# Storing the sums u to DRAM with all 128 rows, and writing the last tokens' row over one of them

## The chip, the cores and the metric

The program runs on one core of a Trainium2 chip. The metric is device time in microseconds (us) of one execution, the median of the runs shown. The engines that appear below are PE (TensorE, matmuls), PEld (its weight loads), DVE (VectorE), ACT (ScalarE), POOL (GpSimd) and SP (SyncE, whose queue issues nearly all DMAs of this kernel, in the order in which they are written). A DMA moves its bytes through up to 16 DMA engines of the core.

## The reference

Attention with two kinds of sparse mask, then a Fourier mixing layer, a normalisation and a feed-forward layer, for 8 batches of 576 tokens and 512 channels:

```python
scores = scale * np.matmul(q, k.transpose(0, 1, 3, 2))
scores = np.where(masks[None, :, :, :], scores, -1000000000.0)
attn = np.exp(scores - np.max(scores, axis=-1, keepdims=True))
x = attn / (np.sum(attn, axis=-1, keepdims=True) + 1e-09) @ v   # to (B, S, H * D)
...
X = np.fft.fft(x, axis=1)
X = np.fft.fft(X, axis=2)
mixed = np.real(X).astype(np.float32)
u = x + mixed
mu = np.mean(u, axis=-1, keepdims=True)
var = np.mean((u - mu) ** 2, axis=-1, keepdims=True)
un = (u - mu) / np.sqrt(var + 1e-06)
ch = np.maximum(un @ w_ch1, 0.0) @ w_ch2
return (u + ch).astype(np.float32)
```

The matrices `q`, `k`, `v` are (8, 8, 576, 64), `w_ch1` is (512, 2048) and `w_ch2` (2048, 512).

## The kernel before

For each batch there are four pairs of heads. A pair is loaded (`qk`, `vn`), its scores are made on PE, masked and exponentiated on DVE and ACT (`sm`, then `pbt` or `qk` as 16-bit parts), transposed by a DMA (`pT`, line 478) and multiplied with the values (PE, lines 490 and 497). The results are stored to DRAM (`xd`, lines 777, 779, 791). When the four pairs of a batch are there, the batch is loaded again in two orders of its tokens (`xa`, `xb`), and matrix products with cosines and sines (`A`, `B`) give the Fourier sum. Its symmetry lets one product serve a token and its mirror image, so the sums `u` come in two halves, "a" and "b", each in two tiles of 128 rows and 512 channels, and a third piece with the last 33 tokens and their mirrors.

The sums are what the change is about. Function `sums` writes them (line 1033 and above) and, for the first two tiles (`t` is 0 or 1), issues a "keep": line 1037 stores the "a" half with all 128 rows to its DRAM tensor `ud`, line 1038 stores the "b" half from row 1 to row 127. Row 0 of "b" is its own mirror and not wanted there. In its place comes the last of the 33 tokens: when the third piece is there (`t` is 2), the step "ux" writes it with a DMA of one row into row 0 of `ud` (line 1045), and the other 32 tokens of both kinds into a tensor that two batches share (lines 1048, 1049). For batches 0 to 2 (`DIRECT`) the sums are normalised from SBUF instead of from `ud`; there line 1044 also writes the row into row 0 of the SBUF tile.

The feed-forward layer takes 18 chunks of 256 rows. For each half of a chunk `u` is loaded (`ul`, line 1281, one buffer), normalised on DVE, POOL and ACT (lines 1075 to 1097), split in two 16-bit parts (`unp`, one buffer) and transposed by a DMA (`uT`, line 1099). Two matrix products follow on PE: `ph` (line 1307) with a relu on ACT (lines 1322, 1323) and a 16-bit remainder on POOL (line 1325), and `acc` (line 1346). DVE adds `u`, loaded once more (`uf`, line 1288), and line 1358 stores the output.

The order of all instructions is made before the program is built: each step is a generator that yields an `op` with an engine, an estimated duration, the rooms it takes and gives back and the names of events that it needs (`need`) or sets (`sets`). A planner picks the next step by estimated time and a priority. The engines then run in the order found; where data must be waited for, a wait on a semaphore is put before the instruction. An SP instruction that waits holds all of SP's queue behind it.

Of the kernel before, what the change touches and what calls it, by code (L numbers as in the profile page):

```python
# [19 lines left out]
B, H, S, D = 8, 8, 576, 64  # L20
# [12 lines left out]
DIRECT = P["dir"]  # L33
# [237 lines left out]
op = Op  # L271
# [3 lines left out]
def body(ctx: ExitStack, tc: tile.TileContext, a, out):  # L275
    nc = tc.nc
# [75 lines left out]
    ud = {key: dram.tile([128, DM], F32, name=f"ud{c}_{i}") for key, (c, i) in place.items()}  # L352
# [406 lines left out]
    def att_out(b, hp, po, eps, scale, xo=None):  # L759
# [4 lines left out]
        if xo is None:  # L764
            xo = apool.tile([128, 2 * NG2 * D], F32, tag="xo", name=f"xo{nm}", bufs=1)
        n = 9 if hp < 2 else 2 * NG2
        sums, vals = po[:, :, :, D], po[:, :, :, 0:D]
        rv = rs[:, 0:n].rearrange("p (a b) -> p a b", a=po.shape[1])
        V.tensor_scalar(rv, sums, eps, scale, op0=ALU.add, op1=ALU.bypass if scale is None else ALU.mult)
        V.reciprocal(rs[:, 0:n], rs[:, 0:n])  # L770
        rb = rv.rearrange("p a (b o) -> p a b o", o=1).to_broadcast([128, po.shape[1], po.shape[2], D])
# [189 lines left out]
    def products32(b, FD, sds, xa, xb):  # L961
# [34 lines left out]
        for t in range(3):  # L996
            r = 128 if t < 2 else 33
            yield op("T", 2.3, get="big" + (" u" if t < 2 else ""), need=" ".join(f"AT{g}_{b}" for g in range(5)), put="f6" if t == 2 else "", note=f"B{t} {b}")
            ps = psbig(f"B{b}_{t}")

            T.matmul(ps[:, 0:512], zerb, zero.to_broadcast([128, 512]), start=True, stop=False)
            both = ps[0:r, 0:512].rearrange("p (i k) -> p i k", i=2)
            for g, (c0, w) in enumerate(GROUPS):
                x = AT[0:w, g, 128 * t : 128 * t + r]
                k0, k1, st = cols[g]
                if g == 0:
                    T.matmul(ps[0:r, 0:257:4], x, tb[0:w, 0:65], start=False, stop=False)
                    T.matmul(ps[0:r, 260:509:4], x, tb[0:w, 1:64], start=False, stop=False)
                elif g < 3:
                    T.matmul(both[:, :, k0:k1:st], x, tb[0:w, c0 : c0 + w].rearrange("p (o k) -> p o k", o=1).to_broadcast([w, 2, w]), start=False, stop=False)  # L1010
                else:
                    T.matmul(both[:, :, k0:k1:st], x, tb[0:w, 257:767].rearrange("p (i k) -> p i k", i=2)[:, :, c0 - 257 : c0 - 257 + w], start=False, stop=False)
            T.matmul(ps[:, 0:512], zerb, zero.to_broadcast([128, 512]), start=False, stop=True)
            spawn(sums(b, t, r, xa, xb, ps[0:r, 0:257], ps[0:r, 256:513], "big"), bias=P["t2"] if t == 2 else None)

    def sums(b, t, r, xa, xb, R_, T_, room):
        tt_ = lambda e, o, x, y, op: e.tensor_tensor(out=o, in0=x, in1=y, op=op)
        for i in range(2):
            o = op("V", 0.92, put=room if i else "", sets="" if b not in DIRECT or not i else (f"u{b}a0", f"u{b}a1", "")[t], note=f"u{t} {b}", alt=None if room == "big" else dict(G=(1.4, P["Lu"])))
            yield o  # L1020
            if i == 0:
                if t < 2:
                    uu = mp.tile([128, 2, DM], F32, tag="u", name=f"u{b}_{t}", bufs=UB)
                    dst = [uu[:, 0], uu[:, 1]]
                else:
                    dst = [xa[0:33, 2], xb[0:33, 2]]
            u, x, lo_, hi_ = (dst[0], xa, R_, T_) if i == 0 else (dst[1], xb, T_, R_)
            if i and room == "big":
                tt_(on(o), u[:, 1:256], lo_[:, 1:256], x[0:r, t, 1:256], ALU.add)
                tt_(on(o), u[:, 0:257:256], hi_[:, 0:257:256], x[0:r, t, 0:257:256], ALU.add)  # L1030
            else:
                tt_(on(o), u[:, 0:257], lo_, x[0:r, t, 0:257], ALU.add)
            tt_(on(o), u[:, 257:512], hi_[:, 255:0:-1], x[0:r, t, 257:512], ALU.add)
        if t < 2:
            us[b, "a", t], us[b, "b", t] = dst
            yield op("S", 1.4, n=2, put="" if b in DIRECT else "u", sets="" if b in DIRECT else f"u{b}a{t} u{b}c{t}", note=f"keep {b} {t}")
            nc.sync.dma_start(ud[b, "a", t], dst[0])
            nc.sync.dma_start(ud[b, "b", t][1:128], dst[1][1:128])
        else:
            yield op("S", 0.4, n=6 if b in DIRECT else 4, put="f6 f6", sets=f"u{b}b0 u{b}b1" + (f" ux{b // 2}" if b % 2 else ""), note=f"ux {b}")  # L1040

            for i in range(2):
                if b in DIRECT:
                    nc.sync.dma_start(us[b, "b", i][0:1], dst[i][32:33])
                nc.sync.dma_start(ud[b, "b", i][0:1], dst[i][32:33])
            hb = 64 * (b % 2)
            ux = ud["x", b // 2]
            nc.sync.dma_start(ux[hb : hb + 32], dst[0][0:32])
            nc.sync.dma_start(ux[hb + 32 : hb + 64], dst[1][0:32])
# [427 lines left out]
```

## Time and profile before

| | |
|---|---|
| median of 3 runs | 1079.88 us (1077.25 to 1080.66) |
| the profiled execution | 1085.56 us |
| its span (first to last instruction) | 1083.8 us |
| PE busy | 958.7 us (88%) |
| DVE, ACT, POOL busy | 561.9, 455.5, 403.5 us |
| mean granted clock of PE | 0.932 of full speed |
| data moved by DMA | 131.23 MB, mean 121 GB/s |

The page cuts the span in 40 slices of 27.1 us and gives for each the busy share of the engines in tenths, the clock that PE was granted and the DMA traffic. The other views used below: the waits (who was idle, and what ended it), the timeline (instructions in order of time with the idle time before them), the chain of work that ended last, the DMA traffic of a stretch, and the busy time of all engines in a list of stretches.

### The profile page before, as it was taken

The numbers are of one execution on the slowest core, as the hardware profiler recorded it, in microseconds if no ns is written. First come the engines' busy times: TensorE is split into PE (matmuls) and PEld (weight loads), VectorE is DVE, ScalarE is ACT, GpSimd is POOL, SyncE is SP. The second block draws the span as 40 slices with busy tenths as digits, with TensorE's granted clock in tenths as the row PEclk, the third lists the DMA queues.
The fourth block names the chain that finished last, engine by engine and source line by source line (L and its number), as shares of the span: only waits on it lengthen the run. The fifth ranks groups of instructions, "written<-read, shape, count | busy, mean of one in ns | idle before, by whom it ended". The sixth has DMA issues, their size and how long they took to land.

```text
span 1083.8 us, 23857 instructions
## 1 busy us (share of the span) xinstructions
PE 958.7 (88%) x9930; PEld 665.8 (61%) x9930; DVE 561.9 (52%) x1040; ACT 455.5 (42%) x893; POOL 403.5 (37%) x389
## 2 busy tenths in 40 slices
PE   7676579896996998977999997899699979999998
PEld 6645464673675666644776665667466656676665
DVE  4777397752864586735873886378616311011000
ACT  3535464442563456534652565356413412222211
POOL 2321132432643373325441654174427323233211
PEclk8858798898998999988999999899889989999999
DMA  8845847607635646258535655674453051130110
GB/s 261 295 163 190 164 134 228 151 31 147 153 103 86 145 119 161 74 137 160 145 75 148 180 121 88 142 198 122 64 143 102 30 93 31 49 78 21 49 40 20
DMA packets 148156, 131.23 MB, mean 121 GB/s; under 512 B 104264, under 2 KB 114760, under 8 KB 148048
## 3 DMA queue, kind: packets, MB, share of 16 engines
q1 hardware_dynamic: 145488, 121.32, 44.6%
q0 software_dynamic: 2560, 8.39, 2.7%
q8 instruction: 78, 1.28, 0.5%
q14 instruction: 30, 0.25, 0.1%
HBM read 79.97 MB, written 28.33 MB: 100 GB/s over the span
## 4 chain that ended last, share of the span: by engine, by line
PE 39%; DMA 7%; DVE 5%; issue 2%; POOL 1%; ACT 1%; SPq 1%; POOLq 0%; DVEq 0%; ACTq 0%
PE acc L1346 18%; PE ph L1307 17%; DMA pT<-pbt 3%; DMA ud<-u 2%; DMA uT<-unp 1%; DVE E L837 1%; PE B L957 1%; DMA ul<-ud 1%; DMA qk<-in_qk 1%; DVE kt L436 1%; PE A L934 1%; PE o L490 0%; PE s L459 0%; DVE FD L837 0%; DMA pT<-qk 0%
## 5 line engine op out<-in xcount | busy, mean ns | idle before, releaser
L1307 PE MATMUL ph<-uT,W 128*128 128x256 f16 x3456 | 399.2, 275 | 12.2 <-DMA uT<-unp 11.6
L1346 PE MATMUL acc<-W,h 128*128 128x512 f16 x1728 | 400.3, 387 | 6.5 <-DVE uf L1354 6.1
L1307 PEld LDWEIGHTS <-W 128*128 128x128 f16 x3456 | 338.2, 99 | 65.2 <-issue 13.2
L1325 POOL TENSOR_TENSOR h<-hf,h 128x512 f16<-128x512 f32 x144 | 181.1, 1257 | 355.3 <-ACT h L1323 271.4
L1346 PEld LDWEIGHTS <-h 128*128 128x128 f16 x1728 | 168.4, 99 | 211.1 <-issue 32.7
L1322 ACT ACTIVATE hf<-ph 128x512 f32<-128x512 f32 x144 | 85.5, 594 | 262.8 <-PE ph L1307 221.8
L1323 ACT ACTIVATE h<-ph 128x512 f16<-128x512 f32 x144 | 85.0, 590 | 0.0
L1097 POOL TENSOR_TENSOR unp<-un,unp 128x512 f16<-128x512 f32 x36 | 44.0, 1222 | 107.5 <-ACT unp L1094 107.4
L1354 DVE SCALAR_TENSOR_TENSOR uf<-acc,cout,uf 128x512 f32<-128x512 f32 x36 | 26.4, 746 | 89.3 <-PE acc L1346 89.2
L436 DVE SCALAR_TENSOR_TENSOR kt<-qk,sc,kt 128x576 f16<-128x576 f32 (+1 forms) x40 | 46.4, 1198 | 31.8 <-ACT kt L421 29.6
L1088 DVE TENSOR_SCALAR un<-ul,mv,rstd 128x512 f32<-128x512 f32 x24 | 20.4, 849 | 80.5 <-POOL rstd L1081 78.8
L1094 ACT CAST unp<-un 128x512 f16<-128x512 f32 x36 | 22.2, 617 | 91.3 <-DVE un L1088 57.7
L1081 POOL TENSOR_TENSOR rstd<-mv,negh 128x1 f32<-128x1 f32 x36 | 23.6, 655 | 96.4 <-DVE mv L1078 66.1
L1075 DVE BATCH_NORM_STATS2 st<-ul 128x6 f32<-128x512 f32 x24 | 16.6, 690 | 75.3 <-DMA ul<-ud 75.3
L837 POOL TENSOR_TENSOR O<-xa,xb 128x1536 f32<-128x1536 f32 x8 | 31.0, 3878 | 15.4 <-DMA xb<-xd,ridx 15.4
L1060 ACT ACTIVATE pq<-B,fcm 128x128 f32<-128x128 f32 (+7 forms) x105 | 27.9, 378 | 19.0 <-PE B L957 8.0
L1181 PE MATMUL gram<-oneb,zero 128*128 128x128 bf16 x379 | 33.4, 261 | 0.0
L421 ACT ACTIVATE kt<-qk,sc 128x576 f16<-128x576 f32 (+1 forms) x40 | 29.3, 784 | 7.3 <-DVE sc L377 6.9
L1181 PEld LDWEIGHTS <-zero 128*128 128x128 bf16 x379 | 30.7, 121 | 2.1 <-issue 1.3
L497 PE MATMUL o<-vsx,pT 54*64 54x65 f16 x720 | 9.1, 208 | 25.2 <-DMA pT<-pbt 25.2
L471 ACT ACTIVATE sm<-sm 128x594 f32<-128x594 f32 (+1 forms) x20 | 16.2, 811 | 35.7 <-DVE sm L754 35.7
L752 DVE TENSOR_REDUCE mx<-sm 128x11 f32<-128x594 f32 (+1 forms) x32 | 29.1, 910 | 0.8
(215 smaller groups left out, 1132.8 us busy)
## 6 DMA issues: line engine op xcount, KB each, us to landing
qk<-in_qk SPq DMA_DIRECT2D x28, 592.0 KB
sa<-in_w SPq DMA_DIRECT2D x20, 512.0 KB
uf<-ud SPq DMA_DIRECT2D x36, 256.0 KB
out<-uf SPq DMA_DIRECT2D x36, 256.0 KB
ul<-ud SPq DMA_DIRECT2D x24, 256.0 KB
vn<-in_vl SPq DMA_DIRECT2D x10, 432.0 KB
W<-in_w SPq DMA_DIRECT2D x8, 512.0 KB
xd<-xo SPq DMA_DIRECT2D x16, 256.0 KB
```

The costliest lines, as they stand in the source:

```text
L421: A.activation(hi, src, AF.Copy, scale=f)
L436: V.scalar_tensor_tensor(out=lo, in0=src, scalar=f, in1=hi, op0=ALU.mult, op1=ALU.subtract)
L752: V.tensor_reduce(out=mx[:, 0:nb], in_=sm, axis=AX.X, op=ALU.max)
L837: tt_ = lambda e, o, x, y, op: e.tensor_tensor(out=o, in0=x, in1=y, op=op)
L1060: A.activation(dst, ps[0:r, c0:c1], AF.Copy, scale=cm[0:r])
L1097: on(o).tensor_tensor(out=unp[:, 1], in0=un, in1=unp[:, 0], op=ALU.subtract)
L1181: T.matmul(idle[-1][:, 0:128], zerb, oneb, start=False, stop=False)
L1307: T.matmul(ph[:, i, :], W1[:, 4 * (f0 // 512) + d, x, f0 % 512 : f0 % 512 + 128], self.uhl[y][:, d, :], start=(n == 0), stop=(n == 11))
L1322: A.activation(hf, ph, AF.Relu, scale=HS)
L1323: A.activation(hh, ph, AF.Relu, scale=HS)
L1325: G.tensor_tensor(out=hl, in0=hf, in1=hh, op=ALU.subtract)
L1346: T.matmul(self.acc[s], (hh, hl)[x][:, i, 128 * s : 128 * s + 128], W2[:, f, 1 - y, :], start=(f == 0 and n == 0), stop=(f == 15 and n == 2))
```

## The change

The "b" half is stored with all 128 rows, as the "a" half is. The row of the last token then goes over row 0 of a tensor that the store has written, so the step "ux" now needs the events that its two keeps are done; for batches 0 to 2 such an event is made, for the others the event was there already. No priority or other number is changed.

```diff
-            yield op("S", 1.4, n=2, put="" if b in DIRECT else "u", sets="" if b in DIRECT else f"u{b}a{t} u{b}c{t}", note=f"keep {b} {t}")
+            yield op("S", 1.4, n=2, put="" if b in DIRECT else "u", sets=f"kept{b}{t}" if b in DIRECT else f"u{b}a{t} u{b}c{t}", note=f"keep {b} {t}")
             nc.sync.dma_start(ud[b, "a", t], dst[0])
-            nc.sync.dma_start(ud[b, "b", t][1:128], dst[1][1:128])
+            nc.sync.dma_start(ud[b, "b", t], dst[1])
         else:
-            yield op("S", 0.4, n=6 if b in DIRECT else 4, put="f6 f6", sets=f"u{b}b0 u{b}b1" + (f" ux{b // 2}" if b % 2 else ""), note=f"ux {b}")
+            kept = f"kept{b}0 kept{b}1" if b in DIRECT else f"u{b}c0 u{b}c1"
+            yield op("S", 0.4, n=6 if b in DIRECT else 4, put="f6 f6", need=kept, sets=f"u{b}b0 u{b}b1" + (f" ux{b // 2}" if b % 2 else ""), note=f"ux {b}")
```

In the built program the order of PE, ACT and SP is the same as before, apart from line numbers (from line 1041 on they are one higher). What changes on SP is the size of the 16 stores and the waits. This is SP at batch 5, where the keep of the second tile and the step "ux" stand side by side (`ud_1_126`, `ud_1_128` are the "a" and "b" halves of the second tile, `u_1_9042` the sums, `xa` and `xb` hold the last tokens; DMAHW names are the semaphores of earlier DMAs). Before:

```order
L1037 DMA ud_1_126<-u_1_9042 128x512 [waits DMAHW1_49,Pool_49]
L1038 DMA ud_1_128<-u_1_9042 127x512 [waits DMAHW2_49,Pool_49]
L1045 DMA ud_0_127<-xa_8079 1x512 [waits DMAHW3_49,DMASW4_49,Pool_49]
L1045 DMA ud_1_128<-xb_8081 1x512 [waits DMAHW4_49,DMASW7_49,DVE_49]
L1048 DMA ud_0_133<-xa_8079 32x512 [waits DMAHW5_49]
L1049 DMA ud_0_133<-xb_8081 32x512 [waits DMAHW6_49]
L478 DMA_TRANSPOSE pT_3_9219<-pbt 128x12x128 [waits DMAHW7_49,DVE_49,PE_49]
```

And the same place of the changed kernel:

```order
L1037 DMA ud_1_126<-u_1_9042 128x512 [waits DMAHW1_49,Pool_49]
L1038 DMA ud_1_128<-u_1_9042 128x512 [waits DMAHW2_49,Pool_49]
L1046 DMA ud_0_127<-xa_8079 1x512 [waits DMAHW3_49,DMAHW6_49,DMASW4_49,Pool_49]
L1046 DMA ud_1_128<-xb_8081 1x512 [waits DMAHW2_49,DMAHW4_49,DMASW7_49,DVE_49]
L1049 DMA ud_0_133<-xa_8079 32x512 [waits DMAHW5_49]
L1050 DMA ud_0_133<-xb_8081 32x512
L478 DMA_TRANSPOSE pT_3_9231<-pbt 128x12x128 [waits DMAHW7_49,DVE_49,PE_49]
```

Nothing has moved; each one-row store has one more wait, for the 128-row store over whose row 0 it writes.

One place moves, on DVE in batch 7 near 867 us (and two instructions of POOL change places there). `uf` is the output of the feed-forward layer, the statistics `st` begin the normalisation of a freshly loaded `ul`. Before:

```order
L1088 TENSOR_SCALAR un_0_11957<-ul_0_11773,mv_0_11841,rstd_0_11892 128x512 [waits DVE_49]
L1354 SCALAR_TENSOR_TENSOR uf_0_11767<-acc_0_11489,cout,uf_0_11767 128x512 [waits DMAHW6_49,DMAHW3_49,PE_49]
L1075 BN_STATS st_1_12012<-ul_1_11969 128x6 [waits DMAHW1_49]
L1076 BN_AGGR mv_1_12013<-st_1_12012 128x2 [waits DVE_49]
L1078 TENSOR_SCALAR mv_1_12013<-mv_1_12013 128x1 [waits DVE_49]
```

And in the changed kernel:

```order
L1089 TENSOR_SCALAR un_0_11957<-ul_0_11773,mv_0_11841,rstd_0_11892 128x512 [waits DVE_49]
L1355 SCALAR_TENSOR_TENSOR uf_0_11767<-acc_0_11489,cout,uf_0_11767 128x512 [waits DMAHW6_49,DMAHW3_49,PE_49]
L1355 SCALAR_TENSOR_TENSOR uf_1_11836<-acc_1_11490,cout,uf_1_11836 128x512 [waits DMAHW4_49,DMAHW0_49,PE_49]
L1076 BN_STATS st_1_12015<-ul_1_11982 128x6 [waits DMAHW1_49]
L1077 BN_AGGR mv_1_12016<-st_1_12015 128x2 [waits DVE_49]
```

The second `uf` now stands before the statistics, which wait for the load of `ul`.

## Rows read from the trace of the kernel before

**Rows 1.** The page: the span and the line of busy time.

```profile
span 1083.8 us, 23857 instructions
PE 958.7 (88%) x9930; PEld 665.8 (61%) x9930; DVE 561.9 (52%) x1040; ACT 455.5 (42%) x893; POOL 403.5 (37%) x389
```

**Rows 2.** The view of waits, of PE: what was to run and what ended the idle time; us in total, times, longest in us.

```profile
PE o L497 <- DMA pT<-pbt: 25.2, 3, 10.3
...
PE ph L1307 <- DMA uT<-unp: 11.6, 1, 11.6
PE t L594 <- ACT pbt L585: 10.7, 1, 10.7
PE n L333 <- ACT jk L402: 8.8, 2, 6.6
PE s L459 <- ACT kt L421: 7.2, 1, 7.2
PE s L518 <- DMA qk<-in_qk: 6.5, 1, 6.5
PE acc L1346 <- DVE uf L1354: 6.1, 1, 6.1
...
PE s L459 <- DVE kt L436: 3.2, 3, 1.3
...
PE o L490 <- DMA pT<-qk: 1.6, 1, 1.6
```

**Rows 3.** The timeline of SP: start in us, how long the instruction held SP, line, operation, tiles.

```profile
96.98 16.85 SPq L1099 DMA_TRANSPOSE uT<-unp  x1
...
115.02 2.20 SPq L1099 DMA_TRANSPOSE uT<-unp  x1
...
236.96 13.80 SPq L1099 DMA_TRANSPOSE uT<-unp  x1
...
333.29 11.30 SPq L1099 DMA_TRANSPOSE uT<-unp  x1
...
447.56 0.26 SPq L1038 DMA_DIRECT2D ud<-u  x1
448.17 8.31 SPq L1045 DMA_DIRECT2D ud<-xa  x1
456.58 2.10 SPq L1045 DMA_DIRECT2D ud<-xb  x1
...
660.01 9.78 SPq L1045 DMA_DIRECT2D ud<-xa  x1
...
768.52 15.45 SPq L478 DMA_TRANSPOSE pT<-pbt  x1
...
858.74 0.61 SPq L1038 DMA_DIRECT2D ud<-u  x1
860.60 8.64 SPq L1045 DMA_DIRECT2D ud<-xa  x1
869.35 0.28 SPq L1045 DMA_DIRECT2D ud<-xb  x1
```

**Rows 4.** The transposes of line 1099 over the whole span: how long each held SP, shortest, median and longest in ns, and the first and last start in us.

```profile
L1099 SPq DMA_TRANSPOSE uT<-unp x36: 1231/1244/16851, 97.0 to 1002.1; - x36
```

**Rows 5.** The DMA view of the stretch from 853.6 to 856.3 us, in 40 slices of 0.07 us: the mean busy share of the 16 DMA engines in tenths, and the traffic. In it stand the keep of batch 7's first tile, line 1037 (issued at 853.6) and line 1038 (issued at 854.3).

```profile
DMA  0000000000005997999979520001002000000105
GB/s 0 0 0 0 0 0 0 0 0 0 0 0 212 394 394 303 425 394 425 364 273 455 182 61 0 30 0 30 0 0 30 0 0 0 30 0 30 30 0 30
```

**Rows 6.** A stretch just after the second keep of batch 3: start and end, length, busy us of PE, PEld, DVE, ACT and POOL with their counts, granted clock, mean busy share of the 16 DMA engines, GB/s.

```profile
450.00:456.00 6.00, 6.00 (x106) 4.09 (x92) 4.34 (x7) 1.29 (x2) 0.58 (x1) 1.00 0.07 27
```

**Rows 7.** The chain of work that ended last, between 555 and 582 us (batch 4's second keep and what follows): start, us, what.

```profile
559.30 17.66 DMA ud<-u
...
577.04 3.89 DMA pT<-qk
```

**Rows 8.** The timeline of the engines: start, us, engine, line, operation, tiles, and in brackets the idle time before it and what ended that.

```profile
105.56 1.16 POOL L1097 TENSOR_TENSOR unp<-un,unp 128x512 f16<-128x512 f32 x1 [9.81 <-ACT unp L1094]
...
122.82 5.14 PE L1307 MATMUL ph<-uT,W 128*128 128x256 f16 x24 [11.58 <-DMA uT<-unp]
...
255.06 0.62 ACT L1094 CAST unp<-un 128x512 f16<-128x512 f32 x1 [13.80 <-DMA uT<-unp]
...
348.85 0.62 ACT L1094 CAST unp<-un 128x512 f16<-128x512 f32 x1 [13.48 <-DMA uT<-unp]
...
661.05 0.76 DVE L475 SCALAR_TENSOR_TENSOR pbt<-sm,pbt 128x594 f16<-128x594 f32 x1
...
680.13 1.21 PE L497 MATMUL o<-vsx,pT 54*64 54x65 f16 x72 [8.96 <-DMA pT<-pbt]
...
787.50 1.21 PE L497 MATMUL o<-vsx,pT 54*64 54x65 f16 x72 [10.30 <-DMA pT<-pbt]
...
878.99 0.69 DVE L1075 BATCH_NORM_STATS2 st<-ul 128x6 f32<-128x512 f32 x1 [11.31 <-DMA ul<-ud]
```

**Rows 9.** Busy time in eight stretches, each just before or after one of the long waits of PE: columns as in Rows 6. The first, the last, and the sum over the eight.

```profile
105.30:111.20 5.90, 5.81 (x73) 5.27 (x73) 1.16 (x1) 2.55 (x5) 3.70 (x3) 0.55 1.70 50
...
880.90:885.40 4.50, 4.50 (x11) 1.57 (x11) 0.40 (x1) 1.69 (x3) 2.27 (x2) 0.50 0.39 105
sum 37.40, PE 35.91 PEld 22.83 DVE 19.21 ACT 12.30 POOL 13.70; mean PE 4.49 PEld 2.85 DVE 2.40 ACT 1.54 POOL 1.71
```

## The prediction

> **What bounds the kernel now.** I began with the page. PE is busy for 958.7 of 1083.8 us [rows 1], so what a change that leaves PE's work alone can win lies in the 125.1 us in which PE stands idle and in what PE's lower clock costs (below). PE's order is the same in the changed kernel, instruction by instruction, so I asked next what ended PE's idle time. The waits of PE [rows 2] show a few long ones, each met once, and they look unrelated: a transposed tile, a load of qk, an ACT copy, a DVE sum. Set side by side with SP's timeline they have one thing in common. Each stands within 30 us behind a keep (lines 1037 and 1038), and in that time one SP instruction holds the queue for 8 to 17 us: a transpose that takes 1.24 us in the median [rows 4] takes 16.85, 13.80, 11.30 or 15.45 us, a store of one row takes 8.31, 9.78 or 8.64 us [rows 3].
>
> Why SP is held is read from the traffic. The keep of 128 rows and the keep of 127 rows move nearly the same bytes. In Rows 5 the first of them shows as a burst: slices of 5 to 9 tenths on 16 engines, at up to 455 GB/s, over in some 12 slices of 0.07 us, 0.8 us. Behind it the store of 127 rows is in flight, and the slices alternate between 0 and 30 GB/s. While two such stores run alone, the mean busy share is 0.07 at 27 GB/s [rows 6], and 0.07 of 16 engines is one engine. At 27 GB/s the 260 KB (127 rows of 2,048 bytes) take 10 us, and two stores one behind the other some 20; the chain of batch 4 has 17.66 us from the second store's issue to what it releases [rows 7]. In that time whatever needs that engine, a transpose or any load that is spread over 16, waits behind it. So sixteen stores each clog one DMA engine for about 10 us, in eight pairs, and SP's queue, which goes in order, stands.
>
> The Trainium skill ("DMA: Bandwidth & Descriptors", the section on why a DMA increments its semaphore by 16) gives a rule for this: a DMA issued from SP is spread over the largest number of engines, up to 16, that divides the size of the slowest dimension on both sides, so 127 rows go to one engine and 128 rows to 16. The trace agrees: 0.07 of 16 engines for 127 rows, and shares up to 0.9 for 128 rows. By that rule the changed store is as quick as its neighbour, and the rival below in which it stays slow has no chance; by the rows alone it keeps a small one.
>
> **What the change takes away, place by place.** I expect each "b" store to look like its "a" neighbour: about 0.8 us of data [rows 5], off SP's path. What PE then no longer waits for (durations of the profiled execution):
>
> Batch 0, two waits, 6.5 and 11.6 us [rows 2]. The load of qk comes without the wait for the clogged engine. For the second wait both transposes count: the first holds SP for 16.85 us from 96.98, the second starts at 115.02 and PE gets its tile at 122.82, 7.8 us later [rows 3, 8]. The second transpose's input is made by POOL from 105.56 to 106.72 [rows 8]; this moves forward about as far as the loads do, some 6 us, so the transpose can start near 101 and land between 105 (3.9 us, the clean transpose of Rows 7) and 109 (the 7.8 us of now, since 512 KB weight loads remain around it). PE comes there at 111.24 minus 6.5, 104.7. I leave 4 us of wait and count 18.1 - 4 = 14. The bounds are 6.5 (only the first wait goes) and 18.1.
>
> Batch 1, 10.7 us, named as ACT's pbt [rows 2]. ACT stood 13.80 us until the transpose gave back the one unp buffer at 255.06 [rows 8]. A transpose at 236.96 that takes 3.9 us lands at 241, so ACT is free 14 us earlier, more than PE waits. All 10.7 go.
>
> Batch 2, 7.2 us and 1.3 behind it, named as ACT's and DVE's kt. The same: ACT waited 13.48 us until 348.85 [rows 8] for a transpose issued at 333.29, which would land near 337, 11 us earlier; the second wait is the longest of DVE's three in Rows 2. 8.5 go.
>
> Batch 3, 6.6 us, ACT's jk [rows 2]: it squares a qk whose load was queued on SP behind one-row stores that held SP for 8.31 and 2.10 us [rows 3]. At 0.4 us each (the quickest one there took 0.28) SP is free 9.6 us earlier, and the wait is 6.6. All goes.
>
> Batch 4, 1.6 us for pT<-qk [rows 2]: issued when the store landed, at 577.04 [rows 7]. It goes.
>
> Batches 5 and 6, 9.0 and 10.3 us [rows 8], two of the three waits in the first line of Rows 2; the third, 25.2 - 19.3 = 5.9 us, stands behind no keep and stays. In batch 5 the operand of the transpose was complete at 661.8 [rows 8], and SP was held until 669.8 by a one-row store [rows 3]. In batch 6 the transpose itself held SP from 768.52 for 15.45 us [rows 3]. With 3.9 us they land at about 666 and 772, and PE comes at 680.13 - 8.96 = 671.2 and at 777.2. Both go, 19.3.
>
> Batch 7, 6.1 us, DVE's uf [rows 2]: DVE stood 11.31 us until ul landed [rows 8], with uf queued behind. SP is free at about 862 instead of 870, and in the new order uf is ahead of that wait. It goes.
>
> Sum: 14 + 10.7 + 8.5 + 6.6 + 1.6 + 19.3 + 6.1 = 66.8 us.
>
> **The clock.** After the long waits PE runs for a while at the lower of its two levels (1.2 instead of 2.4 GHz): in eight stretches at these places it is busy for 35.91 us, at a grant of 0.55 in the first and 0.50 in the last [rows 9]. Half of it, 18.0 us, is what the lower level costs. In batch 0 a short wait remains and the stretch before it, 5.81 us busy, may stay slow; without its half, 2.9, I count 15 us. The bounds are 0 (the grant falls for another reason) and 18.
>
> **What it adds.** 16 rows of 2 KB, nothing. The new waits: each one-row store now waits for a 128-row store. It matters only where the store is issued just ahead, as in batch 3, 5 and 7 (0.6 us before the first row store in batch 3, 1.9 in batch 7 [rows 3]). If a store takes 3 us from issue to landing (the burst of Rows 5 begins 0.8 us after the issue and is over at 1.6; the confirmation I do not see), SP stands 1 to 2.5 us at these three places, with a load of qk, a transpose and a load of ul behind it. By the sums above each comes some 2 to 5 us before PE needs it (in batch 5 at 666 against 671), so I count nothing; without that cover it would be at most 3 x 2.5 = 7.5 us. The Trainium skill ("DMA: Bandwidth & Descriptors", "Anatomy of one DMA", which speaks of DMAs issued by GpSimd) puts the fixed part of a DMA at about 2 us, mostly the confirmation of the last byte; no row here shows that part apart from the rest, and with the burst it would come to the same 3 us.
>
> **The sum.** 66.8 + 15 = 81.8 us. Against the profiled execution's 1085.56 that is 1003.8; the median of the runs is 5.7 us below that execution, which makes 998. Not all waits that come next are visible: PE arrives earlier everywhere, and the steps around it follow only as far as SP, DVE and ACT were themselves held. I take back a tenth, 8 us, and predict 1006.
>
> **The rivals.** (a) Part of it is given back: the freed time is eaten by the next resource in the stage, in batch 0 by the weight loads and DVE, elsewhere by ACT, which has the casts and exponentials of the waiting batch to catch up. For it speaks that DVE and ACT also stand idle during each wait, so their work is dammed up too; against it that they then begin it earlier by the same amount. With batch 0 at its lower bound (6.5), two thirds of the other 52.8 and a third of the clock's 15 the gain is 6.5 + 35 + 5 = 47, so 1033. (b) No change: PE's waits have another cause, and the stores are only near. Against it are eight places out of eight; 1080. (c) Slower: the slowness belongs to the "b" half, its place in SBUF or its tensor, and not to the row count, so 128 rows land as late as 127. Then the new wait holds the second one-row store until 17.66 us [rows 7] after the second keep: in batch 3 447.56 + 17.66 = 465.2 instead of 456.58, in batch 7 876.4 instead of 869.35 [rows 3], later by 8.6 and 7.0 us, and in batch 5, where the same steps stand in the same order, by some 7; all just ahead of waits of PE. 22.6 us on the median give 1103. Such a wait decides from the point where the store's landing lies behind the row's own data. Against it: both halves lie in one tile and go to tensors of the same kind, and only the count of rows differs.
>
> **How the numbers follow.** Two runs of this kernel differ by about 0.3%, 3 us, and less I cannot tell from no change. The forecast has 0.75 with its own range of 988 to 1020 (all of the gaps and the clock, 1079.9 - 66.8 - 4 for what batch 0 may still give - 18 = 991, a little below for what I overlooked, and no gain from the clock: 1079.9 - 60); (a) 0.19, from 1020 to 1050; (b) 0.03; (c) 0.03. The range 988 to 1036 leaves out the slow half of (a), (b) and (c), less than 2 in 10. Faster 0.95, same 0.02, slower 0.03.
>
> **What would show it.** Right: no transpose of line 1099 or 478 holds SP for over 4 us behind a keep, bursts like that of Rows 5 come in twos, PE's waits of Rows 2 are gone but for some 6 us before line 497 and a few in batch 0, and the eight slow stretches are down to two or three. Wrong: a share of 0.07 still stands behind a keep (then (b) or (c)), or the waits of Rows 2 are gone and others of PE with new names stand at the same places (then (a)).

## The result and the profile after

The changed kernel takes 995.08 us (median of 4 runs, 988.72 to 1003.83) against 1080.27 us (1077.25 to 1082.49) of the kernel before, measured beside it: ratio 0.9193, interval 0.9113 to 0.9274. In a second measurement it took 992.49 us against 1079.37 us, ratio 0.9197 (0.9165 to 0.9229). The run of 1003.83 us is a slow one, which the ratio leaves out. The forecast was 1006 us, in a range of 988 to 1036 us.

The profiled execution after took 989.67 us. The lines of the page that answer to [rows 1], and PE's clock in 40 slices:

```profile
span 987.9 us, 23868 instructions
PE 934.8 (95%) x9930; PEld 653.1 (66%) x9930; DVE 564.7 (57%) x1040; ACT 454.8 (46%) x893; POOL 405.4 (41%) x389
...
PEclk9768989999999999999999999999999999999999
```

The span is 95.9 us shorter. PE's idle time, span less busy, fell from 125.1 to 53.1 us, by 72.0; its busy time fell by 23.9 us with the same 9930 instructions. So in this pair of executions three quarters of the gain are waits, and one quarter is work done at a higher clock: from the seventh slice on (148 us) all show 9. (Other executions show less than a quarter; see the clock in the section on the prediction.)

The windows from 83.3 us to the end (columns as in [rows 6]) show where that lies. First the kernel before:

```profile
83.30:1083.80 1000.50, 898.10 (x9165) 616.71 (x9162) 505.97 (x939) 416.86 (x826) 379.71 (x369) 0.95 0.46 111
```

Then the changed kernel:

```profile
83.30:987.90 904.60, 875.18 (x9166) 604.93 (x9166) 508.62 (x939) 416.31 (x827) 381.89 (x369) 0.99 0.46 123
```

Idle is 1000.50 - 898.10 = 102.4 us before and 904.60 - 875.18 = 29.4 us after; in the first 83 us little changed (83.3 - 60.55 = 22.8 us of idle time before, 83.3 - 59.66 = 23.6 after). The waits of PE behind 84 us, in the changed kernel, the longest totals and the one for `qk` (columns as in [rows 2]):

```profile
PE n L333 <- ACT jk L560: 4.5, 2, 3.6
PE gram L1174 <- DVE W L1139: 3.4, 2, 3.2
PE A L935 <- DVE FH L900: 2.8, 4, 1.0
PE n L333 <- ACT jk L402: 2.2, 1, 2.2
PE o L497 <- DMA pT<-pbt: 1.4, 1, 1.4
...
PE s L518 <- DMA qk<-in_qk: 0.4, 1, 0.4
```

No wait above 3.6 us is left, and none for `uT`. The three waits before line 497 that made 25.2 us in [rows 2] are one of 1.4; `jk` of line 402, 8.8 before, is 2.2; `uf`, `kt` of line 421 and ACT's `pbt` are gone.

SP's timeline in batch 6, where a transpose had held SP for 15.45 us [rows 3], now reads (columns as in [rows 3]):

```profile
691.41 0.41 SPq L1037 DMA_DIRECT2D ud<-u  x1
691.91 0.41 SPq L1038 DMA_DIRECT2D ud<-u  x1
694.17 1.88 SPq L478 DMA_TRANSPOSE pT<-pbt  x1
696.22 0.32 SPq L1046 DMA_DIRECT2D ud<-xa  x1
697.44 0.23 SPq L1046 DMA_DIRECT2D ud<-xb  x1
```

And the one-row stores over the whole span, shortest, median and longest in ns; one had taken 9.78 us [rows 3]:

```profile
L1046 SPq DMA_DIRECT2D ud<-xa x8: 245/281/429, 125.3 to 773.3; - x8
L1046 SPq DMA_DIRECT2D ud<-xb x8: 230/236/425, 127.1 to 773.9; - x8
```

The DMA view of batch 7's keeps, from 766 to 770 us in slices of 0.1 us (SP issues the four stores at 766.28, 766.96, 769.02 and 769.69):

```profile
DMA  0000000000099989999989997200000000000049
GB/s 0 0 0 0 0 0 0 0 0 0 0 369 348 389 328 410 348 410 369 410 348 369 389 410 287 62 0 0 0 0 0 0 0 0 0 0 0 0 184 369
```

Where [rows 5] has a burst and then slices of 0 to 30 GB/s, the two stores of the first keep are now one burst of about 1.4 us, over at 768.6, 1.6 us after the second store's issue. Then the engines are empty until the next keep's burst begins at 769.8.

### The profile page after: what moved, and what is told of

It reads as the page before. It is cut to its first block, busy times and chain, and to the rows that moved or that the text cites. A ratio compares the mean times of both kernels' runs of the same rounds, so it can differ in the third digit from the quotient of the medians.

```text
span 987.9 us, 23868 instructions
## 1 busy us (share of the span) xinstructions
PE 934.8 (95%) x9930; PEld 653.1 (66%) x9930; DVE 564.7 (57%) x1040; ACT 454.8 (46%) x893; POOL 405.4 (41%) x389
## 4 chain that ended last, share of the span: by engine, by line
PE 70%; DVE 13%; DMA 7%; issue 4%; POOL 3%; ACT 2%; SPq 1%; DVEq 0%; POOLq 0%; ACTq 0%
PE acc L1347 31%; PE ph L1308 29%; DVE E L837 2%; PE B L957 2%; DMA W<-in_w 2%; PE A L934 1%; DMA uT<-unp 1%; DMA pT<-pbt 1%; POOL xb L827 1%; PE s L459 1%; PE o L490 1%; DVE W L1215 1%; DVE W L1139 1%; DVE kt L436 1%; DVE FD L837 1%
## 5 line engine op out<-in xcount | busy, mean ns | idle before, releaser
L1308 PE MATMUL ph<-uT,W 128*128 128x256 f16 x3456 | 392.5, 273 | 0.0
L1347 PE MATMUL acc<-W,h 128*128 128x512 f16 x1728 | 391.9, 382 | 0.5 <-DMA W<-fs 0.5
L1308 PEld LDWEIGHTS <-W 128*128 128x128 f16 x3456 | 334.8, 98 | 49.1 <-issue 0.2
L1082 POOL TENSOR_TENSOR rstd<-mv,negh 128x1 f32<-128x1 f32 x36 | 22.8, 634 | 76.1 <-DVE mv L1079 44.8
L436 DVE SCALAR_TENSOR_TENSOR kt<-qk,sc,kt 128x576 f16<-128x576 f32 (+1 forms) x40 | 42.8, 1109 | 12.3 <-ACT kt L421 12.2
L837 POOL TENSOR_TENSOR O<-xa,xb 128x1536 f32<-128x1536 f32 x8 | 33.5, 4189 | 17.8 <-DMA xb<-xd,ridx 17.6
L1182 PE MATMUL gram<-oneb,zero 128*128 128x128 bf16 x379 | 30.7, 248 | 0.0
L1174 PE MATMUL gram<-W 128*128 128x128 bf16 x128 | 13.3, 241 | 18.1 <-DVE W L1139 15.8
L1182 PEld LDWEIGHTS <-zero 128*128 128x128 bf16 x379 | 28.1, 114 | 2.2 <-issue 1.4
```

The source lines that it names most:

```text
L436: V.scalar_tensor_tensor(out=lo, in0=src, scalar=f, in1=hi, op0=ALU.mult, op1=ALU.subtract)
L1182: T.matmul(idle[-1][:, 0:128], zerb, oneb, start=False, stop=False)
L1308: T.matmul(ph[:, i, :], W1[:, 4 * (f0 // 512) + d, x, f0 % 512 : f0 % 512 + 128], self.uhl[y][:, d, :], start=(n == 0), stop=(n == 11))
L1347: T.matmul(self.acc[s], (hh, hl)[x][:, i, 128 * s : 128 * s + 128], W2[:, f, 1 - y, :], start=(f == 0 and n == 0), stop=(f == 15 and n == 2))
```

## The experiments

Three theories were open. The first is that of the prediction: a store whose row count is 127 sits on one DMA engine. The second puts it down to the "b" half itself, or to rows that don't begin at 0. The third puts the gain down to the planner, which had new events to plan with and moved two instructions on DVE.

**The "b" half cut in two (e1_split).** The kernel before, with no new wait:

```diff
-            nc.sync.dma_start(ud[b, "b", t][1:128], dst[1][1:128])
+            nc.sync.dma_start(ud[b, "b", t][16:128], dst[1][16:128])
+            nc.sync.dma_start(ud[b, "b", t][1:16], dst[1][1:16])
```

> The kernel before with the b store of rows 1 to 127 cut in two stores, rows 16 to 127 (112 rows) and rows 1 to 15 (15 rows); row 0 is not touched, so the one-row stores get no new wait and no event is added. If the row count decides over how many DMA engines a store is spread (127 rows on one, 112 on 16, 15 on 15): 988 to 1004 us, as the changed kernel, with no transpose that holds SP for over 5 us behind a keep. If it is the b half or the start at row 1 that is slow: 1075 to 1085. If the new waits of the changed kernel cost something, this one is faster than it by 2 to 7 us.

It took 991.16 us (987.59 to 994.21), ratio 0.9188 (0.9156 to 0.922). The rows stored, their source and their tensor are those of the kernel before; only the cut is new, and the whole gain is there. The longest wait of PE behind 84 us is 3.1 us. This run also answers the third theory: it has no new event, and DVE in batch 7 has the order of before (the statistics at 782.99, ahead of the second `uf` at 784.04), yet PE's wait for `uf` is gone too. It is also the measure of the new waits: the changed kernel has them, this one doesn't, and their ratios agree within 0.001, each known to 0.003 or, in the first measurement, 0.008.

One more rival needs a look, since every "b" store ends at row 127: a later start means fewer rows, and the start row (1 here before, 6 and 16 in the cuts) might decide instead of the count. The store of rows 1 to 15 begins at row 1. On one engine its 30 KB would take 1.1 us at 27 GB/s. The DMA view of batch 7's first keep, from 769 to 773 us in slices of 0.1 us:

```profile
DMA  0000000059989999889989943200000000038999
GB/s 0 0 0 0 0 0 0 0 225 471 389 328 389 348 369 308 225 266 266 307 266 328 348 164 123 82 21 0 0 0 0 0 0 0 0 143 328 369 430 369
```

Behind 348 GB/s the traffic of the three stores ends within four slices, on 2 to 4 tenths of the 16 engines, with no stretch of one engine behind it. So a start at row 1 alone does not put a store on one engine. (A store of 127 rows that begins at row 0 was not run.)

**The "a" half with 127 rows (e2_a127).** The changed kernel, its "b" store left whole:

```diff
-            nc.sync.dma_start(ud[b, "a", t], dst[0])
+            nc.sync.dma_start(ud[b, "a", t][1:128], dst[0][1:128])
+            nc.sync.dma_start(ud[b, "a", t][0:1], dst[0][0:1])
```

> The changed kernel, but the a half is stored as rows 1 to 127 and row 0 by itself; the b half stays at 128 rows. If the row count decides: the a store now sits on one engine for 10 us, the waits of PE come back at the same places, 1065 to 1090 us. If it is the b half (its place in the tile, its tensor): 988 to 1010.

It took 1089.48 us (1079.41 to 1092.42), ratio 1.0107 (1.0075 to 1.0139). The whole gain is gone, and the waits of PE stand where they stood in [rows 2], with the same names but for batch 7, the last line here, where PE now waits for ACT's `h`:

```profile
PE o L497 <- DMA pT<-pbt: 22.6, 3, 11.3
...
PE ph L1309 <- DMA uT<-unp: 11.2, 1, 11.2
PE n L333 <- ACT jk L402: 11.1, 2, 8.9
PE t L594 <- ACT pbt L585: 10.8, 1, 10.8
PE s L459 <- ACT kt L421: 7.3, 1, 7.3
PE s L518 <- DMA qk<-in_qk: 6.9, 2, 6.6
PE ph L1309 <- ACT h L1325: 6.8, 1, 6.8
```

Its timeline of SP in batch 1 shows who is held. Line 1038 is here the one-row remainder of "a", line 1039 the full "b" store:

```profile
229.86 9.61 SPq L1038 DMA_DIRECT2D ud<-u  x1
239.56 0.35 SPq L1039 DMA_DIRECT2D ud<-u  x1
240.01 5.69 SPq L1101 DMA_TRANSPOSE uT<-unp  x1
```

And the DMA view of 230 to 240 us, in slices of 0.25 us:

```profile
DMA  8862210000000000000000000000000000000000
GB/s 303 328 238 90 82 57 25 25 25 25 25 33 25 25 25 25 25 25 25 33 25 25 25 25 25 25 25 25 33 25 25 25 25 25 25 25 25 33 25 25
```

The main stall fell on the store of one row that is now next in the queue, and the transpose behind it was held for 5.69 us; in the kernel before the transpose at this place had the whole of it, 13.80 us [rows 3]. Here SP's queue stops at what comes next behind the 127-row store, while 25 GB/s flow, near the 27 of [rows 6]. The half is no cause of its own: "b" is stored whole here and "a" is slow. (It is some 11 us slower than the kernel before. The profiled execution, 1079.41 us, is the fastest of its six, so its trace doesn't show where they come from; the sixteen added one-row stores were not tested by themselves.)

**Only the planner's part (e4_need).** The changed kernel with its events and waits, and the 127-row store of before:

```diff
-            nc.sync.dma_start(ud[b, "b", t], dst[1])
+            nc.sync.dma_start(ud[b, "b", t][1:128], dst[1][1:128])
```

> The changed kernel with the store of 127 rows put back, so that only the planner's part of the change is left (the needed events, and with them uf ahead of the statistics on DVE in batch 7). If the row count is all that counts: 1070 to 1082 us, at most the 6.1 us of batch 7 and some of the slow clock behind it gone. If the new order is what won the time: 990 to 1040.

It took 1074.88 us (1069.38 to 1081.76, 12 runs), ratio 0.9976 (0.9946 to 1.0005). The waits of [rows 2] are there, all but batch 7's: instead of 6.1 us for `uf` PE waits 2.6 us. DVE's timeline there:

```profile
861.88 0.75 DVE L1355 SCALAR_TENSOR_TENSOR uf<-acc,cout,uf 128x512 f32<-128x512 f32 x1 [0.55 <-PE acc L1347]
872.63 0.70 DVE L1076 BATCH_NORM_STATS2 st<-ul 128x6 f32<-128x512 f32 x1 [10.00 <-DMA ul<-ud]
```

`uf` now stands ahead of the wait for `ul`, which is nearly as long as in [rows 8] (10.00 against 11.31 us). The 3.9 us between the medians fit the 3.5 us by which that wait of PE shrank, but the interval reaches past 1: of the planner's part this says that it is worth a few us at most, and it isn't settled that it is worth any. The order alone doesn't remove the wait: e2_a127 has the same order, DVE waits 14.28 us for `ul` there, and PE waits 6.8 us; and e1_split, without this order, has no wait at that place.

**122 rows (e3_122).** The kernel before, cut at row 6:

```diff
-            nc.sync.dma_start(ud[b, "b", t][1:128], dst[1][1:128])
+            nc.sync.dma_start(ud[b, "b", t][6:128], dst[1][6:128])
+            nc.sync.dma_start(ud[b, "b", t][1:6], dst[1][1:6])
```

> The kernel before with the b store cut in rows 6 to 127 (122 rows, 2 times 61) and rows 1 to 5. If a store is spread over the largest number up to 16 that divides its rows: two engines, so half as long (about 5 us each at 27 GB/s per engine, a pair 10) and a mean share of 0.13 while it runs alone. Most of PE's waits were shorter than the delay that caused them, so most of them should be gone with half the delay: 1000 to 1030 us, with what is left in batch 0 and 6. If any store whose rows are no multiple of 16 sits on one engine: 1075 to 1085.

It took 1004.52 us (1002.09 to 1007.85), ratio 0.9322 (0.9292 to 0.9353). The Trainium skill ("DMA: Bandwidth & Descriptors", the section on why a DMA increments its semaphore by 16) spreads a DMA over the largest number up to 16 that divides the slowest dimension: two engines for 122 rows. The DMA view of batch 6's two keeps, 697 to 712 us in slices of 0.375 us, bears it out:

```profile
DMA  0098130113559998882112112159999111111112
GB/s 0 38 360 306 33 33 11 44 38 66 87 147 322 350 322 295 322 295 93 60 60 93 55 51 54 50 127 126 114 130 58 55 49 55 49 49 55 49 45 44
```

Behind the second burst it falls to 44 to 60 GB/s in most slices, twice the 27 of [rows 6]. The transpose of this place, on SP's timeline:

```profile
704.36 6.24 SPq L478 DMA_TRANSPOSE pT<-pbt  x1
```

It holds SP for 6.24 us, between the 15.45 of before [rows 3] and 1.88. Of PE's wait of 10.30 us [rows 8] 3.0 are left at this place (the longest of the second line below), and of the 11.6 in batch 0 5.7:

```profile
PE ph L1308 <- DMA uT<-unp: 5.7, 1, 5.7
PE o L497 <- DMA pT<-pbt: 4.4, 2, 3.0
...
PE n L333 <- ACT jk L402: 2.2, 1, 2.2
```

So the dose decides, and not in proportion: two engines in place of one bring 74 us where 16 bring some 87. At the other places of [rows 2] PE's wait is gone altogether.

**One batch at a time (e5_only0, e6_only6, e7_only4).** The changed kernel with the 127-row store in one batch, B = 0, 6 or 4:

```diff
-            nc.sync.dma_start(ud[b, "b", t], dst[1])
+            r0 = 1 if b == B else 0
+            nc.sync.dma_start(ud[b, "b", t][r0:128], dst[1][r0:128])
```

> The changed kernel with the store of 127 rows for batch 0 alone. By the terms of the prediction batch 0 is worth 14 us of PE's waits and some 2 of slow clock: 16 us slower than the changed kernel, two waits of 6 and 11 us near 99 and 111 us of the span. If what was won there is eaten by the weight loads behind it: under 8 us.

> The changed kernel with the store of 127 rows for batch 6 alone. By the terms of the prediction: a wait of 10.3 us before line 497 and 2.9 us of slow clock, 13 us slower than the changed kernel. If the places feed on each other (a wait in one batch makes room in the next): clearly less, under 8.

> The changed kernel with the store of 127 rows for batch 4 alone. By the terms of the prediction: 1.6 us slower than the changed kernel, since SP is held as long as elsewhere and PE hardly waits. If a held SP costs PE its time wherever it stands: 8 to 15 us.

The changed kernel ran beside them once more (e8_after_again).

> The changed kernel once more, for comparison on the same chip as the three kernels with one slow batch: 988 to 1004 us.

| 127 rows in | us | ratio to before | more than e8_after_again |
|---|---|---|---|
| none (e8_after_again) | 992.49 | 0.9197 (0.9165 to 0.9229) | |
| batch 0 (e5_only0) | 1006.82 | 0.9349 (0.9309 to 0.939) | 14.3 |
| batch 6 (e6_only6) | 1007.06 | 0.9333 (0.9306 to 0.936) | 14.6 |
| batch 4 (e7_only4) | 998.45 | 0.9252 (0.9218 to 0.9286) | 6.0 |

Each slow store brings back the waits of its own place. PE's waits with batch 0 alone:

```profile
PE ph L1309 <- DMA uT<-unp: 11.3, 1, 11.3
PE s L518 <- DMA qk<-in_qk: 6.8, 2, 6.6
...
PE o L497 <- DMA pT<-pbt: 2.5, 1, 2.5
```

With batch 6 alone, first SP's timeline:

```profile
698.52 15.78 SPq L478 DMA_TRANSPOSE pT<-pbt  x1
```

And PE's, the next matmul of line 497:

```profile
718.16 1.21 PE L497 MATMUL o<-vsx,pT 54*64 54x65 f16 x72 [11.43 <-DMA pT<-pbt]
```

Batch 6 costs 14.6 us for a wait of 11.43, so some 3 us beyond the wait, where the two intervals leave 4.5 us on either side (5.6 for batch 0). (The last line of batch 0's waits belongs to another place; the explanation below comes back to it.) Batch 4 shows a wait of 1.6 us before line 490, as in [rows 2], and its median is 6.0 us longer; the two intervals leave about 5 us on either side of that difference (half-widths 0.0034 and 0.0032 of some 1079 us, added in squares), so 1.6 is just inside, and whether something else in batch 4 costs time isn't settled. The trace shows no other wait of PE from 495 to 560 us. It does show waits of 1.7 us at 106.5, 1.5 at 144.1 and 2.7 at 455.0 that e8_after_again doesn't have; they stand ahead of the slow store, issued at 505.0, so it did not cause them, and single traces differ by as much.

## Why the prediction was right, step by step

- **The mechanism** held at every step: one engine per 127-row store, SP held behind it, PE waiting late for a transpose or a load. e1_split and e2_a127 leave neither rival (c) nor (b). (a) came only in batch 0, where a wait with a new name stands at the old place, 3.2 us.
- **The waits, 66.8 us.** PE's idle time after the opening stage fell by 73.0 us. Two places explain most of the difference. The third wait before line 497, 5.9 us, which "stands behind no keep and stays", shrank to 1.4 us: 4.5 us too little counted. It lies between the keeps of batches 3 and 4, some 50 us behind the nearest, and is 2.5 us in e5_only0, where only batch 0 has a slow store. Among kernels in which all batches have one it is 6.8 us in e4_need and 2.5 in e2_a127, so it does not follow the slow stores alone. Why it shrank no run tells. The other place is batch 0.
- **Batch 0, 14 us.** 18.1 less the 3.2 us that remain is 14.9. That the size was right is luck, since the reason is another than the one given. PE no longer waits there for the transpose, as was reckoned, but for DVE, which makes the weights of line 1139:

```profile
104.56 0.41 PE L1174 MATMUL gram<-W 128*128 128x128 bf16 x4 [3.16 <-DVE W L1139]
105.16 0.86 PE L1174 MATMUL gram<-W 128*128 128x128 bf16 x12 [0.19 <-DVE W L1139]
105.97 2.78 PE L1308 MATMUL ph<-uT,W 128*128 128x256 f16 x24
```

  The product with `uT` follows at 105.97 without a wait. The experiment gives 14.3 us for this place, clock and all, and 5.6 either way.
- **Batches 5 and 6, 19.3 us, batch 7, 6.1, and the rest** went as worked out. In batch 7 the step named two causes, a free SP and the new order of DVE. A free SP is enough: the wait is gone in e1_split without the new order, and with the order but a held SP 2.6 and 6.8 us of wait were left (e4_need, e2_a127).
- **The clock, 15 us,** was about right, though the two profiled executions above seem to say that it was sized too small: there PE's busy time fell by 23.9 us. The step took eight short stretches, 35.91 us of PE in 37.40 [rows 9]. In that trace of the kernel before ten longer stretches at the lower level have no counterpart in the trace after. Their sum, in the columns of [rows 6]:

```profile
sum 92.40, PE 47.48 PEld 30.92 DVE 36.23 ACT 27.67 POOL 26.24; mean PE 4.75 PEld 3.09 DVE 3.62 ACT 2.77 POOL 2.62
```

  Half of 47.48 is 23.7 us, as measured between these two. But the execution before lay 5.3 us above its median of 1080.27, and the one after 5.4 below its own. Two more profiles have nearly the waits of before (e2_a127, e4_need), two more nearly those of after (e1_split, e8_after_again). Their lines of busy time, in this order:

```profile
PE 950.4 (88%) x9927; PEld 661.2 (61%) x9930; DVE 561.2 (52%) x1040; ACT 455.6 (42%) x893; POOL 404.7 (38%) x389
PE 950.8 (89%) x9927; PEld 662.9 (62%) x9930; DVE 563.4 (53%) x1040; ACT 455.1 (42%) x893; POOL 402.0 (38%) x389
PE 939.6 (95%) x9927; PEld 656.6 (66%) x9930; DVE 560.9 (57%) x1040; ACT 455.2 (46%) x893; POOL 407.6 (41%) x389
PE 936.4 (95%) x9927; PEld 655.6 (66%) x9930; DVE 562.2 (57%) x1040; ACT 454.8 (46%) x893; POOL 405.0 (41%) x389
```

  With the pair above, the mean of the three with long waits is 953.3 us and of the three without 936.9. The difference of 16.4 us is an estimate from six executions of five kernels; it is close to the 15 us of the prediction and inside its bounds of 0 and 18. The prediction got near it by way of one trace, in which the eight stretches were cut close at their edges.
- **The new waits, nothing,** held: e1_split, without them, is as fast. SP does stand for 3.7, 2.1 and 3.3 us ahead of the first one-row store of batches 3, 5 and 7, but for 3.2, 2.0 and 2.8 in e1_split too, where that store waits for the row's own data alone. So the new wait adds some 0.5 us at most.
- **A tenth taken back, 8 us,** was not lost. This step made most of the miss: without it the sum 81.8 would have given 998, and the medians differ by 85.2 us in the first measurement and 86.9 in the second. What the traces show comes to the same: 72.0 us of waits and the 16.4 of the clock are 88. (Between the two profiled executions it is 95.9, with 23.9 for the clock.)

## What to carry to other kernels

Look at a store's row count before its bytes: a DMA of 127 rows ran at 27 GB/s on one engine, one of 128 rows at some 400 on 16. The cost shows elsewhere, as waits with unrelated names, each within some 30 us behind such a store; set the long waits of the bound engine beside the timeline of the queue that issues, and look for an instruction that is ten times its median. Where no row may be spared, cut the piece so that its bulk is a multiple of 16 rows: the cut was as good here as writing a row too many and overwriting it.

## What was not expected of the hardware

- Two engines are much more than half of the way: 122 rows, whose stores run at some 50 GB/s, took 13 us more than the cut at row 16; 127 rows cost some 87. The text ahead of that run had 1000 to 1030 us, on the ground that most of PE's waits are shorter than the delay behind them.
- PE ran at the lower of its two levels around a single wait of 11.43 us, which went with 14.6 us of time. The window of e6_only6 from 711.8 to 722.1 us, columns as in [rows 6]:

```profile
711.80:722.10 10.30, 3.94 (x86) 3.07 (x87) 0.46 (x2) 0.00 (x0) 0.00 (x0) 0.50 0.53 103
```

  At a grant of 0.50, half of the 3.94 us of PE is what the level costs: 2.0 us, with the wait 13.4. In e8_after_again, without the wait, the grant is 1.00 from 690 to 720 us. The rest is within the 4.5 us that the two intervals leave open.
